# Sliding-window attention with a gated MLP on one core: q and k of batches 2 to 7 in runs of eight rows, sorted by VectorE, turned by one DMA transpose each

## The chip, the cores and the metric

The kernel runs on one core of a Trainium2 chip. The time is the device time of one execution in microseconds. A core has five engines that each run their own program in order: TensorE (in the profile PE, its weight loads PEld), VectorE (DVE), ScalarE (ACT), GpSimd (POOL) and SyncE (SP). They wait for each other through semaphores. DMA transfers are issued from SP, ACT or GpSimd and run on 16 DMA engines that all queues share.

## What is computed

q, k and v are 8 x 8 x 576 x 64 (batches, heads, rows, head size). Attention looks back over a window of 64 rows; its output, as 4608 rows of 512, goes through a two-layer MLP whose hidden values h become h * cos(h).

```
scores = scale * np.matmul(q, k.transpose(0, 1, 3, 2))
rel = pos[:, None] - pos[None, :]
mask = (rel >= 0) & (rel < window)
scores = np.where(mask, scores, -1000000000.0)
...
attn = np.exp(scores)
attn = attn / (np.sum(attn, axis=-1, keepdims=True) + 1e-09)
return np.matmul(attn, v).astype(np.float32)
...
h = x @ w_in
g = h * np.cos(h)
return (g @ w_out).astype(np.float32)
```

w_in is 512 x 2048, w_out 2048 x 512.

## The kernel before

**Tiles.** The MLP runs in nine macro tiles (mt 0 to 8) of 512 rows. Each has an h phase, in which PE makes 16 blocks of 128 hidden features (h_ps, four matmuls each, L458), ACT takes the sine (L597) and DVE multiplies h by it into gT (L600), and an out phase of 64 matmuls (out_ps, L611) whose results are copied and stored. The h blocks go round five PSUM banks, so a block's bank is taken again five blocks later. Attention works on batches of 576 rows; a batch has nine blocks j of 64 queries, each against 128 keys (block j - 1 and block j), and four pairs of heads. In tile mt the scores of batch mt + 1 are made, so that their results are there when the next tile takes its attention output (o_ps, values) as xT, the MLP's input.

**A batch's way.** For batches 2 to 7, `load_chunk` (L162) loads q and k on GpSimd's queue in six chunks of 96 rows for all heads, casting to bf16. `turn_k` (L238) turns each k chunk with a DMA transpose on SP's queue into kT, which holds head dimension on partitions and rows in order along the free axis. q is turned by PE: `transposed` (L193, L203) writes tq_ps in PSUM, one transpose of 96 columns per chunk and pair, and `put_q` (L213) has DVE copy it into qT. For batches 4 to 6 two of the six q chunks, and for batch 7 all six, go by DMA instead (`turn_q`, L226, `TURNED`, L40). `burst_scores` (L275) then issues the scores of several groups at once: 72 matmuls a batch (L289) in two bursts, of 32 and 40. The rhs is k as `keys` (L270) cuts it out; for even j the two chunks of 64 keys are read in reverse order. After that a group of four units goes through DVE (add of the mask with a minimum, L326), ACT (exp, L338), DVE (reciprocal, L348), GpSimd (the product w, L355) and a DMA transpose of w on SP's queue (L374; a few groups are transposed by PE, L371).

**Batches 0 and 1** are loaded by `load_heads` in runs of nine rows and turned by PE; their reordering is done when PSUM is copied. They and tile 0 are written out by hand in a list of steps (`FIRST`, L44 to L63), which also sets the first loads of batch 2 (Lq2, Lk2).

**The order of the rest** is a plan: `at(time, function, ...)` (L482) enters a step, and `pump(time)` (L485) emits all steps that are due. Time counts in units: tile mt begins at T * mt with T = 32, the h phase has units 0 to 15 (one per block), the out phase 16 to 31 (four matmuls each). The bursts are due at units 14.6 and 20.2 (the very first at 15.5), the work on a score group follows its place in the burst, the xT copies (`put_x`) come from 31.2 on. Lines 510 to 531 enter the loads, turns and spreads of each batch. The engines execute what is emitted for them in this order, and a step that must wait holds up what stands behind it on its engine.

**The start.** `make_identity` (L546; GpSimd, masks.py) comes first, then the list: `io` (iota on GpSimd, L127), the loads of the first pair of heads over SP, the masks made by DVE (`mk`) and cast by ACT (`mc`), the casts of the first rows, and then GpSimd's loads of the other pairs (L149).

## Time and profile before

| | us |
|---|---|
| median of 3 runs | 305.95 |
| lowest and highest | 305.73, 306.08 |
| span of the profiled execution | 304.8 |

| DMA queue | packets | MB | share of 16 engines |
|---|---|---|---|
| q0, issued from GpSimd | 100192 | 18.06 | 80.8% |
| q1, issued from SP | 57808 | 22.66 | 40.7% |

The span runs from the first to the last instruction of one execution, and the time of a run is a little longer than it. An engine's busy time is the time in which it executes something; a row of the stage view gives a stretch, its length and the busy time of each engine with the count of its instructions. The chain of waits follows the end of the program back to its start: each piece has its start, its length and the work that the rest waited for. A row of the group view has line, engine, operation, output and inputs with shapes, a count, then busy time in us and mean ns of one, then idle time of the engine just before and what ended it.

### The profile page before, as it was taken

How to read it: one execution, taken by the hardware profiler on the slowest of the kernel's cores; microseconds unless marked ns; L12 is line 12 of the kernel's file. 1: busy time of each engine (PE TensorE's matmuls, PEld its weight loads, DVE VectorE, ACT ScalarE, POOL GpSimd, SP SyncE). 2: the span in 40 equal slices, each digit the busy share in tenths (PEclk: the TensorE clock that was granted, in tenths of full speed). 3: DMA queues.
4: the chain of work that ended last, by engine and by line, in shares of the span. 5: the costliest groups of instructions: out<-in, count | busy, mean ns of one | idle time of the engine just before them, and what ended most of it. 6: DMA issues, size and time to landing. Idle time of an engine off the chain costs nothing.

```text
span 304.8 us, 8261 instructions
## 1 busy us (share of the span) xinstructions
PE 293.2 (96%) x2840; PEld 154.4 (51%) x2840; DVE 217.4 (71%) x868; ACT 233.7 (77%) x783; POOL 195.8 (64%) x226
## 2 busy tenths in 40 slices
PE   3789999999999999999999999999999999999995
PEld 3667854644455445444544444444544454454443
DVE  3797888898888877787678867886778677236701
ACT  5998699878986799779976998699869986116500
POOL 8899568986999579985998599769804930000000
PEclk9999999999999999999999999999999999999999
DMA  7999999999979995999999999999996852011011
GB/s 144 175 203 184 196 189 142 103 132 169 232 115 115 228 147 80 106 153 233 133 116 150 223 138 109 128 235 148 107 123 147 139 120 98 0 71 69 3 69 69
DMA packets 158186, 41.44 MB, mean 136 GB/s; under 512 B 146944, under 2 KB 153408, under 8 KB 158144
## 3 DMA queue, kind: packets, MB, share of 16 engines
q0 software_dynamic: 100192, 18.06, 80.8%
q1 hardware_dynamic: 57808, 22.66, 40.7%
q8 instruction: 22, 0.36, 0.5%
q14 instruction: 20, 0.16, 0.2%
q10 hardware_dynamic: 144, 0.20, 0.2%
HBM read 36.70 MB, written 9.44 MB: 151 GB/s over the span
## 4 chain that ended last, share of the span: by engine, by line
PE 90%; DVE 3%; DMA 2%; POOL 2%; ACT 1%; issue 1%; POOLq 0%
PE h_ps L458 37%; PE out_ps L611 36%; PE out_ps L441 5%; PE h_ps L422 4%; PE s_ps L289 3%; PE o_ps L390 3%; DMA k<-in_k_dram 2%; PE tq_ps L203 1%; PE out_ps L470 1%; DVE negm L321 1%; POOL q L149 1%; PE s_ps L311 1%; POOL k L149 1%; ACT e L338 0%; DVE wT L121 0%
## 5 line engine op out<-in xcount | busy, mean ns | idle before, releaser
L458 PE MATMUL h_ps<-xT,w_in 128*128 128x512 bf16 x512 | 115.1, 379 | 0.2
L611 PE MATMUL out_ps<-w_out,gT 128*128 128x512 bf16 x496 | 110.0, 379 | 0.0
L600 DVE TENSOR_TENSOR gT<-h_ps,sin 128x512 bf16<-128x512 f32 x128 | 85.1, 688 | 29.3 <-ACT sin L597 28.7
L338 ACT ACTIVATE e<-s,negm 128x128 f32<-128x128 f32 (+1 forms) x256 | 97.2, 382 | 1.7 <-POOL v L121 1.0
L597 ACT ACTIVATE sin<-h_ps 128x512 f32<-128x512 f32 x128 | 73.8, 598 | 31.4 <-PE h_ps L458 30.8
L355 POOL TENSOR_TENSOR w<-e,rden 128x512 bf16<-128x512 f32 (+1 forms) x68 | 69.3, 1033 | 30.8 <-DVE rden L348 25.0
L458 PEld LDWEIGHTS <-w_in 128*128 128x128 bf16 x512 | 48.9, 98 | 54.7
L611 PEld LDWEIGHTS <-gT 128*128 128x128 bf16 x496 | 47.4, 98 | 56.1
L326 DVE CUSTOM_DVE_ANT_0 s<-s_ps,mask 128x128 f32<-128x128 f32 (+1 forms) x256 | 56.1, 277 | 1.7 <-PE s_ps L311 1.4
L338 ACT ACTIVATION_READ_ACCUMULATOR e<-s,negm 128x1 f32 x256 | 48.3, 189 | 0.0
L172 POOL DMA_DIRECT2D v<-in_v_dram x40 | 34.1, 870 | 1.0 <-DMA q<-in_q_dram 1.0
L166 POOL DMA_DIRECT2D q<-in_q_dram x36 | 28.7, 797 | 7.6 <-DMA v<-in_v_dram 2.5
L166 POOL DMA_DIRECT2D k<-in_k_dram x36 | 28.5, 792 | 6.4 <-DMA k<-in_k_dram 4.5
L121 ACT COPY out_sb<-out_ps 128x512 f32<-128x512 f32 (+1 forms) x16 | 9.0, 563 | 23.9 <-PE out_ps L611 18.4
L348 DVE RECIPROCAL rden<-den 128x4 f32<-128x4 f32 (+1 forms) x73 | 12.2, 167 | 19.4 <-ACT e L338 19.0
L121 POOL COPY v<-v 64x1536 bf16<-64x1536 bf16 (+3 forms) x16 | 22.9, 1433 | 0.4
L121 DVE COPY out_sb<-out_ps 128x512 f32<-128x512 f32 x20 | 13.7, 687 | 12.1 <-PE out_ps L611 12.0
L121 DVE CAST xT<-o_ps 128x512 bf16<-128x512 f32 x24 | 15.6, 679 | 8.6 <-PE o_ps L390 8.4
L326 DVE DVE_READ_ACCUMULATOR2_ANT negm<- 128x1 f32 x256 | 21.3, 83 | 0.1
L441 PE MATMUL out_ps<-w_out,gT 128*128 128x512 bf16 x64 | 14.8, 380 | 0.0
L422 PE MATMUL h_ps<-xT,w_in 128*128 128x256 bf16 x128 | 14.6, 273 | 0.0
L422 PEld LDWEIGHTS <-w_in 128*128 128x128 bf16 x128 | 12.3, 98 | 1.4
(67 smaller groups left out, 230.9 us busy)
## 6 DMA issues: line engine op xcount, KB each, us to landing
out_dram<-out_sb SPq DMA_DIRECT2D x16, 512.0 KB, 7.3
v<-in_v_dram POOLq DMA_DIRECT2D x32, 128.0 KB, 6.0
q<-in_q_dram POOLq DMA_DIRECT2D x36, 96.0 KB, 8.7
k<-in_k_dram POOLq DMA_DIRECT2D x36, 96.0 KB, 8.6
w_in<-in_moe_w_in_dram POOLq DMA_DIRECT2D x4, 512.0 KB, 9.2
w_out<-in_moe_w_out_dram POOLq DMA_DIRECT2D x4, 512.0 KB, 11.0
q<-in_q_dram POOLq DMA_DIRECT2D x7, 144.0 KB, 6.5
k<-in_k_dram POOLq DMA_DIRECT2D x7, 144.0 KB, 6.7
```

What stands on the lines that cost most here:

```text
L121: {"a": nc.scalar.copy, "p": nc.gpsimd.tensor_copy}.get(engine, nc.vector.tensor_copy)(out, in_)
L166: nc.gpsimd.dma_start(out=st[name, b][:, c].rearrange("p (h d) -> p h d", h=H), in_=src.rearrange("h p d -> p h d"))
L172: nc.gpsimd.dma_start(out=vt.rearrange("p (h d) -> p h d", h=H), in_=v[b, :, c * 128:c * 128 + n, :].rearrange("h p d -> p h d"))
L326: nc.vector.tensor_tensor_reduce(out=s[:, u, c], in0=s_ps[:, u, c], in1=mask[:, 2 - j % 2 if j else 0, c], scale=-scale if b else -1.0, sc ...
L338: nc.scalar.activation(e[:, u, c], s[:, u, c], AF.Exp, bias=negm[:, u:u + 1], scale=1.0 if n < n_first else -1.0, accum_out=den[:, u:u + 1])
L355: (nc.gpsimd if engine == "p" else nc.vector).tensor_tensor(out=w[:, 0:u], in0=e[:, 0:u], op=ALU.mult, in1=rden[:, 0:u].unsqueeze(2).to_br ...
L422: nc.tensor.matmul(out=h_ps[:, half * e:half * e + half], lhsT=w_in_sb[:, ks, ff * 128:ff * 128 + 128], rhs=st["xT", 0][:, ks, half * g:ha ...
L441: nc.tensor.matmul(out=st["out", m], lhsT=st["g", ff // 2][:, ff % 2, m * 128:m * 128 + 128], rhs=w_out_sb[:, ff], start=ff == 0, stop=ff ...
L458: nc.tensor.matmul(out=st["h", ff], lhsT=w_in_sb[:, ks, ff * 128:ff * 128 + 128], rhs=st["xT", mt][:, ks], start=start, stop=stop)
L597: nc.scalar.activation(sin, h_ps, AF.Sin, bias=math.pi / 2.0)
L600: nc.vector.tensor_tensor(out=gt[:, e], in0=h_ps, in1=sin, op=ALU.mult)
L611: nc.tensor.matmul(out=o_ps[e], lhsT=gT[ff // 2][:, ff % 2, ms * 128:ms * 128 + 128], rhs=w_out_sb[:, ff], start=ff == 0, stop=ff == n_ff - 1)
```

## The change

- `load_chunk` gives way to `load_runs`: q or k of a batch is loaded in two parts of four heads, each partition taking eight successive rows of a head (72 partitions, 2 KB of the source in one piece).
- `sort_runs` (new, DVE): each part is copied into sorted_rows, 80 partitions by 8 by 512, so that the free axis goes first over the row's place in its run, then over heads and head dimension. Partitions 64 to 79 are zeroed once, on GpSimd.
- `turn` (new, SP): one DMA transpose turns all of sorted_rows (80 x 4096). k's result is kT itself, now [128, 8, 4, 80]: place in the run, pair, run. q's result is q_turned, a new tile with one buffer.
- `put_runs` (new, GpSimd): four copies a batch put q in row order into qT.
- `keys` and the burst's matmul: k is read in the order place in the run, then run (eight neighbouring elements, then a step of 320), and the output is written with a step of eight elements to put the columns in order.
- The PE transposes and copies of q for batches 2 to 7, `turn_q`, `turn_k` and `TURNED` are gone. Loads, sorts, turns, put_runs and the loads of v have new places in the plan; batches 2 and 3 have places of their own.

```diff
-NC, NP = 6, 96
+RUN, NP = 8, 80
+RUNS = (0.8, 0.6), (22, 9), (23.3, 10.3)
+RUNS3 = (1, 7), (28.4, 22), (29.5, 23.3)
-TURNED = {4: 2, 5: 2, 6: 2, 7: 6}
...
-    "Lq2.0 Ge.11 Gi.10 Gm.14 g.1.7 Lq2.1 Lq2.2 o.0.1.2 ...
+    "Lq2.0 Ge.11 Gi.10 Gm.14 g.1.7 Lq2.1 o.0.1.2 ...
...
-    "X.3.d Gm.18 o.3.3 oc.3.d Ge.18 Gn.17.d Lk2.4 Gi.18 Gn.18.d Lk2.5 Lv1.4 "
+    "X.3.d sq.0 sq.1 uq Gm.18 o.3.3 oc.3.d Ge.18 Gn.17.d Gi.18 Gn.18.d Lv1.4 "
...
+    sorted_rows = const.tile([NP, RUN, d_model], BF16, name="sorted_rows")
...
-    def load_chunk(name, b, c):
-        if (name, b) not in st:
-            st[name, b] = rows_tile(name)[0:NP].rearrange("p (c x) -> p c x", c=NC)
-        src = {"q": q, "k": k}[name][b, :, c * NP:c * NP + NP]
-        nc.gpsimd.dma_start(out=st[name, b][:, c].rearrange("p (h d) -> p h d", h=H),
-                            in_=src.rearrange("h p d -> p h d"))
+    def load_runs(name, b, part):
+        n = H // 2
+        st[name, b, part] = rows = rows_tile(name)[0:S // RUN, 0:n * RUN * D].rearrange("p (h x) -> p h x", h=n)
+        src = {"q": q, "k": k}[name][b, n * part:n * part + n]
+        nc.gpsimd.dma_start(out=rows, in_=src.rearrange("h (p r) d -> p h (r d)", r=RUN))
+
+    def sort_runs(name, b, part):
+        n = H // 2
+        to = sorted_rows[0:S // RUN, :, n * D * part:n * D * part + n * D]
+        nc.vector.tensor_copy(to.rearrange("p r (h d) -> p r h d", h=n),
+                              st.pop((name, b, part)).rearrange("p h (r d) -> p r h d", r=RUN))
...
-        else:
-            for c in range(TURNED.get(b, 0) if name == "q" else 0, NC):
-                nc.tensor.transpose(t_ps[:, NP * c:NP * c + NP], of[:, c, 128 * p:128 * p + 128], ident[:NP, :NP])
...
-    def turn_q(b, c):
-        nc.sync.dma_start(out=qsets[b % 2][:, :, c * NP:c * NP + NP], in_=st["q", b][:, c], transpose=True)
+    def turn(name, b):
+        if name == "k":
+            to = k_tile(b)
+        else:
+            st["q", b] = to = att.tile([128, RUN, PAIRS, NP], BF16, tag="q_turned", name="q_turned", bufs=1)
+        nc.sync.dma_start(out=to.rearrange("d r a x -> d (r a) x"), in_=sorted_rows.rearrange("p r x -> p (r x)"), transpose=True)
+
+    def put_runs(b, p):
+        of = st["q", b][:, :, p, 0:S // RUN]
+        nc.gpsimd.tensor_copy(qsets[b % 2][:, p].rearrange("d (x r) -> d x r", r=RUN), of.rearrange("d r x -> d x r"))
...
-            st["kA", b] = ka = att.tile([128, PAIRS, S], BF16, tag="kT", name="kT", bufs=2)
+            st["kA", b] = ka = att.tile([128, RUN, PAIRS, NP], BF16, tag="kT", name="kT", bufs=2)
...
-    def turn_k(b, c):
-        nc.sync.dma_start(out=k_tile(b)[:, :, c * NP:c * NP + NP], in_=st["k", b][:, c], transpose=True)
...
+        if b > 1:
+            rhs = st["kT", b, p][:, :, lo // RUN:lo // RUN + 64 // RUN * chunks]
+            rhs = rhs.rearrange("d r (a t) -> d a r t", a=chunks)
+            return rhs[:, ::-1] if j and j % 2 == 0 else rhs, chunks
...
-                        nc.tensor.matmul(out=to.rearrange("p (a t) -> p a t", a=chunks),
+                        nc.tensor.matmul(out=to.rearrange("p (a t r) -> p a r t", a=chunks, r=RUN),
...
-        for c in range(TURNED.get(b, 0)):
-            at(t0 - T + (24.3 if b == 4 else 23.4 if c < 2 else 26.4) + 0.01 * c, turn_q, b, c)
-        for p in range(PAIRS if TURNED.get(b) != NC else 0):
-            t_q = t0 + (2 if b == 2 else 1) + (3.3 if b == 2 else 3.5) * p
-            at(t_q, tr_q, b, p)
-            at(t_q + 0.02, put_q, b, p)
         if b > 2:
-            for c in range(NC):
-                for i, name in enumerate(("q", "k")):
-                    at(t0 - T + (17.9 + 2.8 * i if b == 3 and c == NC - 1 else 5.6 + 1.6 * c + 0.8 * i), load_chunk, name, b, c)
-        for c in range(NC):
-            at(t0 + 0.1 * c - (2 if b == 2 else 6), turn_k, b, c)
+            loads, sorts, turns = (RUNS3 if b == 3 else RUNS)
+            for i, name in enumerate("qk"):
+                for part in range(2):
+                    at(t0 - T + loads[i] + 0.1 * part, load_runs, name, b, part)
+                    at(t0 - T + sorts[i] + part, sort_runs, name, b, part)
+                at(t0 - T + turns[i], turn, name, b)
+        for p in range(PAIRS):
+            at(t0 + (7 if b == 2 else 5 if b == 3 else 3.3) + p, put_runs, b, p)
         for c in range(5):
-            at(t0 + (8 if TURNED.get(b) == NC else 0.5) + c, load_v, b, c)
+            at(t0 + 7.6 + c, load_v, b, c)
...
+    for part in range(2):
+        at(T + 5.4 + part, sort_runs, "k", 2, part)
+    at(T + 6.5, turn, "k", 2)
...
     make_identity(nc, ident)
     nc.vector.memset(small, 0.0)
+    nc.gpsimd.memset(sorted_rows[64:NP], 0.0)
     exp_table()
```

In this notation t0 = T * (b - 1) is the tile in which batch b's scores are made, and t0 - T the one before it.

More of the change, by code (lines that the diff above doesn't have):

```diff
@@ L195, in transposed, with in_order @@
         of = st[name, b]
-        if b < 2:
-            for c in range(RC):
-                for h in range(2):
-                    d = slice(64 * h, 64 * h + 64)
-                    nc.tensor.transpose(t_ps[d, 64 * c:64 * c + 64], of[d, p, 64 * c:64 * c + 64], ident[d, d])
-        else:
-            for c in range(TURNED.get(b, 0) if name == "q" else 0, NC):
-                nc.tensor.transpose(t_ps[:, NP * c:NP * c + NP], of[:, c, 128 * p:128 * p + 128], ident[:NP, :NP])
-        return t_ps
-    def in_order(t_ps, to, b):
-        return (t_ps.rearrange("d (c p) -> d p c", c=RC), to.rearrange("d (p c) -> d p c", c=RC)) if b < 2 else (t_ps, to)
+        for c in range(RC):
+            for h in range(2):
+                d = slice(64 * h, 64 * h + 64)
+                nc.tensor.transpose(t_ps[d, 64 * c:64 * c + 64], of[d, p, 64 * c:64 * c + 64], ident[d, d])
+        return t_ps
+    def in_order(t_ps, to):
+        return t_ps.rearrange("d (c p) -> d p c", c=RC), to.rearrange("d (p c) -> d p c", c=RC)
     def tr_q(b, p):
@@ L213, in put_q @@
     def put_q(b, p, engine=None):
-        if b > 1:
-            lo = TURNED.get(b, 0) * NP
-            copy(engine, qsets[b % 2][:, p, lo:], st.pop(("tq", b, p))[:, lo:])
-            return
-        of, to = in_order(st.pop(("tq", b, p)), qsets[b][:, p], b)
+        of, to = in_order(st.pop(("tq", b, p)), qsets[b][:, p])
         if b:
@@ L570 @@
              "c": lambda p, g, engine: g_put(2 * p + g, engine), "v": values_half, "x": put_x_half,
-             "tb": sine_table, "tb2": exp_table, "h": first_half, "S": sine_half, "g": gate_half,
+             "sq": lambda part: sort_runs("q", 2, part), "uq": lambda: turn("q", 2), "tb": sine_table, "tb2": exp_table, "h": first_half, "S": sine_half, "g": gate_half,
              "Gs": g_scores, "Gm": g_max, "Ge": g_exp, "Gi": g_inv, "Gn": g_norm, "Gw": g_trans, "Gc": g_trans,
```

15 lines of the change are left out of this document (8 added, 7 removed), and 6 rows, old and new, of the table FIRST.

## The prediction

> **What bounds the kernel now.** I read the page's engine shares first, then the busy time by stage, then the chain of waits, then the instruction groups with their shapes kept apart. A stage here is one macro tile: from its first h_ps matmul to the next tile's.
>
> ```profile
> span 304.8 us, 8261 instructions
> PE 293.2 (96%) x2840; PEld 154.4 (51%) x2840; DVE 217.4 (71%) x868; ACT 233.7 (77%) x783; POOL 195.8 (64%) x226
> ```
>
> ```profile
> core 0: us, PE busy (x) PEld busy (x) DVE busy (x) ACT busy (x) POOL busy (x), PEclk, DMA share, GB/s
> 57.50:89.30 31.80, 31.80 (x297) 15.89 (x295) 27.35 (x120) 27.12 (x100) 27.31 (x32) 1.00 1.99 163
> 89.30:120.80 31.50, 31.48 (x288) 15.59 (x289) 23.97 (x111) 27.28 (x95) 25.39 (x29) 1.00 1.41 140
> ...
> 152.00:183.20 31.20, 31.15 (x280) 15.27 (x281) 23.66 (x111) 27.10 (x95) 25.92 (x29) 1.00 1.58 155
> ...
> 214.40:244.90 30.50, 30.44 (x265) 14.57 (x265) 22.87 (x107) 27.09 (x95) 16.78 (x17) 1.00 0.92 127
> ```
>
> PE fills each tile and its clock is full, so a microsecond taken from PE in a tile is a microsecond gained, and any other engine matters only once it makes PE wait. The last row is tile 7, whose batch already has no q transpose on PE: 30.50 us, where tile 5 (with 16 of them) takes 31.20. That is the change's own experiment, made within the kernel before. The chain of waits says the same, and shows a second thing, the start:
>
> ```profile
> 0.78 0.18 POOL ident masks.py:197
> 0.96 0.07 issue
> 1.02 0.29 POOL ident masks.py:199
> 1.31 0.20 POOL mask L127
> ...
> 1.80 0.70 POOL q L149
> ...
> 5.87 6.71 DMA k<-in_k_dram
> ...
> 27.64 10.59 PE h_ps L422 x96
> ...
> 60.12 0.26 PE tq_ps L203 x6
> ...
> 85.13 0.22 PE tw_ps L371 x4
> ...
> 154.75 0.17 PE tq_ps L203 x4
> ...
> 166.68 0.52 PE s_ps L289 x32
> ...
> 172.48 0.80 PE s_ps L289 x40
> 173.28 8.74 PE out_ps L611 x40
> ```
>
> Until 5.87 us the chain is GpSimd alone, in its program's order: identity, iota, loads. From 26 us on it is almost only PE. So a delay at the head of GpSimd's program is carried to the end, because nothing behind it has slack. The last row also gives the planner's unit (four out_ps matmuls): 8.74 / 10 = 0.87 us.
>
> **The change part by part.** The rows that carry prices:
>
> ```profile
> L203 PE MATMUL tq_ps<-ident,q 96*128 96x96 bf16 x96 | 7.4, 205 | 0.0
> L121 DVE COPY qT<-tq_ps 128x576 bf16<-128x576 bf16 x12 | 6.4, 544 | 0.0
> L121 DVE COPY qT<-tq_ps 128x384 bf16<-128x384 bf16 x12 | 4.2, 347 | 0.0
> L121 DVE COPY v<-v 64x2048 bf16<-64x2048 bf16 x1 | 1.1, 1124 | 0.0
> L121 POOL COPY v<-v 64x512 bf16<-64x512 bf16 x2 | 2.0, 1012 | 0.1
> L166 POOL DMA_DIRECT2D q<-in_q_dram x36 | 28.7, 797 | 7.6 <-DMA v<-in_v_dram 2.5 <-PE tk_ps L200 1.6 <-DMA q<-in_q_dram 1.4
> L149 POOL DMA_DIRECT2D q<-in_q_dram x7 | 4.0, 578 | 0.5 <-DMA q<-in_q_dram 0.5
> masks.py:197 POOL MEMSET ident<- 128x128 bf16 x1 | 0.2, 205 | 0.3 <-POOLq L635 0.3
> L635 POOL MEMSET const-bfloat16-1.0<- 128x1 bf16 x1 | 0.1, 102 | 0.0
> L600 DVE TENSOR_TENSOR gT<-h_ps,sin 128x512 bf16<-128x512 f32 x128 | 85.1, 688 | 29.3 <-ACT sin L597 28.7
> L597 ACT ACTIVATE sin<-h_ps 128x512 f32<-128x512 f32 x128 | 73.8, 598 | 31.4 <-PE h_ps L458 30.8
> ```
>
> *Transposes removed from PE.* All 96 of L203 go. On the chain six take 0.26 us and four 0.17, so 0.043 us each: 96 x 0.0433 = **-4.16 us**. The stage rows agree: 31.20 - 30.50 = 0.70 for 16.
>
> *A memset added at the head of GpSimd's program.* The 16 spare partitions of sorted_rows, 4096 bf16 each, are zeroed right behind the identity, ahead of iota and every load. The two memset rows give (205 - 102) / 127 = 0.81 ns per element of a partition, so 0.10 + 4096 x 0.81 ns = 3.4 us. Lower end 0.1 us (the one-element row, if length cost nothing), upper end 6.6 (205 / 128 ns for each element). I take 3.4, since the 128-element row is this very operation, with this type, on this engine. DVE's masks wait for the iota, q's and k's first casts are queued behind them, and PE for both; every load shifts too. Nothing covers it: **+3.4 us**.
>
> *Loads.* Twelve chunk loads per batch at 0.797 become four; with 0.58 (the L149 row, long runs as well) GpSimd saves 9.6 - 2.3 = 7.3 us per batch. GpSimd's queue is not on the path after the start, so this earns nothing.
>
> *put_runs.* Four copies of 128x576 per batch on GpSimd. No row has its stepped read; the nearest copy takes 1.01 us at 512 elements, so some 1.1, and 2.2 at twice that. 4 x 1.1 = 4.4 us, less than the loads give back. It runs at units 3.3 to 6.3 and the scores come at 14.6, so 8 units (7 us) cover it; at 2.2 each it ends some 9 us after its start at unit 3.3, still before 14.6. Without that cover a score burst would wait. Nothing in the sum, 0 to +1 in the range.
>
> *Sorts on DVE.* Four copies of 72x2048 per batch replace four copies of qT. The nearest row is v's 64x2048: 1.12 us. DVE gains 4.5 and loses 1.4 (4 x 0.347) per tile, 23.7 + 3.1 = 26.8 of 30.5. In the h phase DVE gates each h_ps block.
>
> ```profile
> 160.09 0.69 DVE L600 TENSOR_TENSOR gT<-h_ps,sin 128x512 bf16<-128x512 f32 x1 [0.17 <-ACT sin L597]
> ```
>
> The block's bank (one of five) is needed again 4 x 0.87 = 3.5 us after PE leaves it; sin takes 0.60, the gate 0.69, with some 0.2 between, so slack is about 2.0 us. A k pair at units 9 and 10 delays by 2 x 1.12 less the 0.26 per block by which DVE is faster (0.60 apart against 0.87): 1.7. It fits, barely, so nothing in tiles 2 to 6.
>
> The Trainium skill, "VectorE: DVE Perf Modes", the tier table, gives a bf16 copy within SBUF four elements per cycle, 693 ns for 2048 elements. By that the pair would be far inside the slack; this trace's 2048 row took 1124 ns and does not show the faster rate.
>
> *Turns.* SP gets two large transposes for the six of k and the q chunks.
>
> ```profile
> kT<-k SPq DMA_TRANSPOSE x36, 5.0
> ```
>
> ```profile
> L239 SPq DMA_TRANSPOSE kT<-k x36: 1182/1216/2490, 59.3 to 228.2; - x36
> ```
>
> ```profile
> q1 hardware_dynamic: 57808, 22.66, 40.7%
> ```
>
> One turn moves 80 x 4096 x 2 = 655 KB. q1 moved 22.66 MB in 40.7% of 16 engines' 304.8 us, 183 KB per us with all of them, so 3.6 us of data. Issue on SP: at least 1.2 us, at most 9.7 if it goes by column blocks (32 against four). Landing after issue: 5.0 us (the chunk's median, which already holds queueing), 12 at worst. Queued behind the turn on SP are weight transposes and stores; the q turn of batch 4 stands ahead of the transpose of batch 3's block 4 (unit 24.2), due at 31, so there 0 taken, +4 in the range. In the steady tiles the sorted_rows buffer is reused 11.7 and 17.7 units (10 and 15 us) after a turn, so DVE does not wait. Two places are tight:
>
> ```profile
> 59.16 0.69 DVE L355 TENSOR_TENSOR w<-e,rden 128x512 bf16<-128x512 f32 x1
> 60.86 2.48 DVE L600 TENSOR_TENSOR gT<-h_ps,sin 128x512 bf16<-128x512 f32 x4 [1.00 <-ACT sin L597]
> ```
>
> Tile 1: batch 2's q sorts come right before it, 2.2 us on a DVE that has 1.0 us to spare; the first gate slips 1.2, of which some 0.6 is slack (PE asks for the first bank again around 62.1, the gate ends at 61.5). The k sorts at units 5.4 and 6.4 find DVE already late: 0.3 more. **+0.9 us** (0 to 3: batch 2's k turn at 6.5 is due at 15.5, 7.8 us). End of tile 1: batch 3's k turn goes out near unit 24.4 and lands 5.0 us, 5.8 units, later, at 30.2; the q sort placed at 28.4 needs the buffer and waits, then both sorts take 2.6 units, to 32.8. The xT copies behind them, due from 31.5, are 1.3 units late: **+1.1 us** (0 to 5).
>
> *Scores with strides.* 72 matmuls per batch read k in 16-byte runs and write every eighth PSUM column. They take 0.52 + 0.80 = 1.32 us per batch, 18 ns each since four run side by side. No row has a stepped access on PE. Lower end: nothing. Upper end: each alone, as the w transposes of the same 128 columns run (0.22 / 4 = 55 ns): 72 x 37 ns = 2.7 us per batch, 16 in all. I take nothing: the row nearest in kind is the same burst, where even blocks already read the two chunks in reverse with no price visible.
>
> The Trainium skill, "PSUM — Partial Sum Buffer", Specifications (TRN2), says the opposite: PSUM's lines are 8 bytes and any non-contiguous pattern slows matmuls significantly. No run here shows it yet; it gives no figure, and what it would do is the second rival.
>
> **Sum.** -4.16 + 3.4 + 0.9 + 1.1 = +1.2 us, on the span 304.8: 306.0. The runs' median lies 305.95 - 304.8 = 1.15 above the profiled span, so **307.2 us**, with 305.0 to 309.0 as this case's own range.
>
> **The rivals.**
>
> First, *the start absorbs the memset* (the other side). If the memset is far shorter than its length says, or the first loads catch up because fewer transfers stand beside them, the shift is near nothing: 307.2 - 3.4 = 303.8, and 302 where the tight places hold too. It decides once the shift is below 1.5 us. For it: the first two loads come over SP and do not shift. Against: the chain's first 5.9 us run through GpSimd without a gap.
>
> Second, *stepped scores stream at half rate.* The place is every burst, on PE. Doubled, they cost 1.32 x 6 = 7.9 more: 315.1; with only half of that 311. For it: nothing hides it, since PE is full. Against: only that no row shows a price. This is what the PSUM page's sentence would come to here.
>
> Third, *the sorts make PE wait in every tile.* If a sort also waits for its load or for the buffer, by 3 us where the slack left is 0.3 to 2, each of tiles 2 to 6 loses some 1.2: 313. For it: DVE is at 26.8 of 30.5 and the k pair almost uses up the slack. Against: 10 us between uses of the buffer.
>
> **How the numbers follow.** About 0.2% (0.6 us) is what this kernel's measurement can tell from no change. The forecast has 0.42 (0.03 faster, 0.12 within, 0.27 slower), the first rival 0.28 (0.26 faster, 0.02 within), the second 0.22 and the third 0.08 (all slower). That makes 0.29 faster, 0.14 the same, 0.57 slower. The range 302.6 to 312.5 leaves out a start that costs nothing beside tight places that hold, and the full doubling of the scores.
>
> **What would show it.** The first GpSimd load starts at 5.2 us and not 1.8 (memset right); PE's steady row after the start begins some 3 us later. Tiles 2 to 6 take 30.5 us each with no s_ps growth; 31.8 each would be the doubled score burst, visible as 1.0 and 1.6 us pieces on the chain. An idle DVE with a DMA as releaser at the end of tile 1, or an h_ps matmul waiting for DVE in tile 1, shows the two stalls. I am wrong if the memset is short, if strides cost PE, or if the sorts hold back gates in steady tiles.

## The result and the profile after

The changed kernel takes 348.36 us (median of 4 runs, 345.64 to 350.51), the kernel before 305.98 beside it: 1.137 times as long, with a 95% interval of 1.133 to 1.141. That is 42 us slower, where 1.2 were forecast and the range ended at 312.5. Executions of one version can lie some per cent apart at a lower granted clock, so where they lie more than 1.5% apart the faster ones are read: 347.72 us (and not 357.09) for e6, 327.82 (and not 334.46) for e11, 318.31 and 319.00 (and not 326.64 and 328.27) for e13.

First the page of the kernel after, its span and engine shares, and the shares of its chain of waits:

```profile
span 347.3 us, 7972 instructions
PE 303.7 (87%) x2744; PEld 157.4 (45%) x2744; DVE 226.7 (65%) x872; ACT 233.8 (67%) x783; POOL 191.7 (55%) x203
...
PE 37%; DMA 36%; POOL 11%; issue 5%; DVE 5%; ACT 4%; DVEq 0%; POOLq 0%
```

PE was 96% busy before and is 87% busy now; the program's end is set by transfers as much as by PE. PE also has 10.5 us more busy time for fewer instructions, to which the clock and the step in PSUM come back below. The view by stage, each row from a tile's first h_ps matmul to the next tile's (tiles mt 1, 2 and 6; the prediction called mt 4 "tile 5" and mt 6 "tile 7", and from here on the program's own numbers stand):

```profile
core 0: us, PE busy (x) PEld busy (x) DVE busy (x) ACT busy (x) POOL busy (x), PEclk, DMA share, GB/s
60.10:113.20 53.10, 36.05 (x273) 17.30 (x272) 30.80 (x128) 28.06 (x101) 23.57 (x24) 0.90 0.95 111
113.20:151.59 38.39, 31.99 (x264) 15.54 (x264) 26.45 (x111) 27.25 (x96) 24.81 (x25) 1.00 1.20 156
...
255.57:287.43 31.86, 31.62 (x265) 15.36 (x265) 22.95 (x107) 28.45 (x100) 24.18 (x23) 1.00 0.65 101
```

Subtracting the same stages of the kernel before gives where the 42.5 us between the two spans come from: the start +2.7, tile 1 +21.1, tile 2 +6.9, tiles 3 to 6 +3.6, +2.9, +4.0 and +1.3, and nothing in tiles 7 and 8, which no longer make scores. Half of the loss is in one tile. The chain of waits of the kernel after shows what is in it (start, length, work):

```profile
1.37 3.50 POOL sorted_rows L558
5.44 0.69 POOL q L151
...
60.92 14.61 DMA q_turned<-sorted_rows
75.62 0.69 DVE sorted_rows L173
76.31 0.61 DVE gT L611
76.97 1.10 PE h_ps L467 x3
78.06 12.31 DMA kT<-sorted_rows
90.41 1.71 PE s_ps L298 x32
...
269.88 0.89 PE s_ps L298 x32
...
276.06 1.43 PE s_ps L298 x40
```

Read it from 60.92. Batch 2's q turn takes 14.61 us. VectorE's sort of k needs the same buffer and stands in DVE's program ahead of gates; it can start at 75.62. The gate behind it, and the h_ps matmuls that want its bank, wait with it. Then k's turn goes out at 78.06 and lands 12.31 us later, and only then can the scores begin. The view of waits of the kernel after (engine, line, what it waited for: us in total, times, longest) shows that these waits are everywhere that a turn's end is needed:

```profile
POOL qT L234 <- DMA q_turned<-sorted_rows: 18.2, 2, 13.6
DVE sorted_rows L173 <- DMA kT<-sorted_rows: 16.6, 5, 4.6
...
PE h_ps L467 <- DVE gT L611: 10.1, 4, 5.2
...
PE s_ps L298 <- DMA kT<-sorted_rows: 8.2, 1, 8.2
...
DVE sorted_rows L173 <- DMA q_turned<-sorted_rows: 6.6, 1, 6.6
```

GpSimd's wait of 13.6 us stands in tile 1 too: `put_runs` waits for the q turn, and batch 3's k loads and batch 2's v loads are queued behind it. They go out from 77.3 us on, so they run beside the k turn of 78.06: one late turn makes the next one late. The turns themselves, by the transfer rows of the kernel after (median us from issue to landing) and by the view of their line (ns to issue one on SP: least, median, most):

```profile
q_turned<-sorted_rows SPq DMA_TRANSPOSE x6, 5.9
kT<-sorted_rows SPq DMA_TRANSPOSE x6, 13.8
```

```profile
L230 SPq DMA_TRANSPOSE q_turned<-sorted_rows x6: 3203/3426/6222, 60.9 to 251.1; - x6
L230 SPq DMA_TRANSPOSE kT<-sorted_rows x6: 3404/6416/8818, 78.1 to 235.2; - x6
...
DMA to landing us min/median/max: 5.6/10.7/15.6
```

The twelve turns, set beside the times at which GpSimd's loads are issued and land, fall into groups. Five have none of these loads beside them, or only the end of one, and land in 5.6 to 5.9 us. Six have four to seven of them beside them and land in 12.3 to 15.6. One (113.3 us), whose four loads start 1.6 us after it, takes 9.1. It isn't a matter of q or k: batch 3's k turn (103.85, no load beside it) takes 5.8, batch 2's q turn 14.6.

### The profile page after: what moved, and what is told of

The parts are those of the page before. It is cut to its first block, busy times and chain, and to the rows that moved or that the text cites. A ratio compares the mean times of both kernels' runs of the same rounds, so it can differ in the third digit from the quotient of the medians.

```text
span 347.3 us, 7972 instructions
## 1 busy us (share of the span) xinstructions
PE 303.7 (87%) x2744; PEld 157.4 (45%) x2744; DVE 226.7 (65%) x872; ACT 233.8 (67%) x783; POOL 191.7 (55%) x203
## 4 chain that ended last, share of the span: by engine, by line
PE 37%; DMA 36%; POOL 11%; issue 5%; DVE 5%; ACT 4%; DVEq 0%; POOLq 0%
PE h_ps L467 16%; PE out_ps L622 14%; DMA kT<-sorted_rows 13%; DMA k<-in_k_dram 7%; DMA w_out<-in_moe_w_out_dram 6%; DMA v<-in_v_dram 5%; DMA q_turned<-sorted_rows 4%; ACT e L347 4%; POOL w L364 4%; PE out_ps L450 3%; POOL v L123 2%; DVE sorted_rows L173 2%; PE s_ps L298 2%; PE out_ps L479 1%; POOL sorted_rows L558 1%
## 5 line engine op out<-in xcount | busy, mean ns | idle before, releaser
L467 PE MATMUL h_ps<-xT,w_in 128*128 128x512 bf16 x512 | 117.7, 391 | 12.3 <-DVE gT L611 10.1
L622 PE MATMUL out_ps<-w_out,gT 128*128 128x512 bf16 x496 | 110.9, 382 | 0.0
L611 DVE TENSOR_TENSOR gT<-h_ps,sin 128x512 bf16<-128x512 f32 x128 | 83.3, 686 | 29.7 <-ACT sin L608 29.6
L608 ACT ACTIVATE sin<-h_ps 128x512 f32<-128x512 f32 x128 | 73.4, 599 | 41.4 <-PE h_ps L467 34.9
L467 PEld LDWEIGHTS <-w_in 128*128 128x128 bf16 x512 | 51.3, 100 | 76.2 <-issue 20.4
L234 POOL COPY qT<-q_turned 128x576 bf16<-128x576 bf16 x24 | 28.8, 1247 | 18.2 <-DMA q_turned<-sorted_rows 18.2
L179 POOL DMA_DIRECT2D v<-in_v_dram x40 | 35.6, 901 | 1.0 <-DMA k<-in_k_dram 0.5
L123 DVE COPY out_sb<-out_ps 128x512 f32<-128x512 f32 x20 | 13.7, 686 | 15.1 <-PE out_ps L622 14.5
L298 PE MATMUL s_ps<-kT,qT 64*64 64x128 bf16 (+1 forms) x432 | 15.5, 312 | 8.2 <-DMA kT<-sorted_rows 8.2
L173 DVE COPY sorted_rows<-q 72x2048 bf16<-72x2048 bf16 x12 | 9.4, 819 | 16.6 <-DMA kT<-sorted_rows 16.6
L357 DVE RECIPROCAL rden<-den 128x4 f32<-128x4 f32 (+1 forms) x73 | 12.0, 165 | 11.4 <-ACT e L347 11.0
L399 PE MATMUL o_ps<-wT,v 128*64 128x64 bf16 x512 | 11.0, 197 | 8.6 <-POOL v L123 3.6
L298 PEld LDWEIGHTS <-qT 64*64 64x64 bf16 x432 | 12.2, 141 | 13.2 <-issue 13.2
## 6 DMA issues: line engine op xcount, KB each, us to landing
q<-in_q_dram POOLq DMA_DIRECT2D x12, 288.0 KB, 11.4
```

The source lines that it names most:

```text
L123: {"a": nc.scalar.copy, "p": nc.gpsimd.tensor_copy}.get(engine, nc.vector.tensor_copy)(out, in_)
L173: nc.vector.tensor_copy(to.rearrange("p r (h d) -> p r h d", h=n), st.pop((name, b, part)).rearrange("p h (r d) -> p r h d", r=RUN))
L179: nc.gpsimd.dma_start(out=vt.rearrange("p (h d) -> p h d", h=H), in_=v[b, :, c * 128:c * 128 + n, :].rearrange("h p d -> p h d"))
L234: nc.gpsimd.tensor_copy(qsets[b % 2][:, p].rearrange("d (x r) -> d x r", r=RUN), of.rearrange("d r x -> d x r"))
L298: nc.tensor.matmul(out=to.rearrange("p (a t r) -> p a r t", a=chunks, r=RUN), lhsT=qsets[b % 2][d, pe, 64 * j:64 * j + 64], rhs=rhs[d], st ...
L467: nc.tensor.matmul(out=st["h", ff], lhsT=w_in_sb[:, ks, ff * 128:ff * 128 + 128], rhs=st["xT", mt][:, ks], start=start, stop=stop)
```

## The experiments

A theory stood at the start: a turn lands in 12 to 15 us beside GpSimd's loads, and load, sort, turn and put form one chain through one buffer, which has no lead. The rivals were the memset, the stride on PE, and sorts that are simply too long. Each ratio is to the kernel before measured beside that run (306.85 to 307.37 us). The table has the length of each tile in us, worked out from the starts of the tiles' first h_ps matmuls in the traces.

| kernel | median us | tile 1 starts | 1 | 2 | 3 | 4 | 5 | 6 |
|---|---|---|---|---|---|---|---|---|
| before | 305.98 | 57.4 | 32.0 | 31.5 | 31.2 | 31.2 | 31.2 | 30.5 |
| after | 348.36 | 60.1 | 53.1 | 38.4 | 34.7 | 34.1 | 35.2 | 31.9 |
| e1_memset_late | 342.44 | 56.3 | 55.5 | 36.4 | 32.5 | 34.9 | 33.7 | 31.9 |
| e2_two_buffers | 336.20 | 59.8 | 45.3 | 37.9 | 31.5 | 31.5 | 37.8 | 31.5 |
| e3_no_v | 336.57 | 60.9 | 52.1 | 34.2 | 31.5 | 31.5 | 33.0 | 31.5 |
| e4_out_plain | 346.45 | 60.4 | 54.8 | 37.1 | 33.8 | 33.8 | 33.8 | 30.8 |
| e5_loads3_late | 332.76 | 60.1 | 43.0 | 36.2 | 32.9 | 31.5 | 34.2 | 31.9 |
| e6_read_steps | 347.72 | 60.2 | 54.6 | 35.9 | 33.8 | 33.9 | 33.9 | 33.6 |
| e7_v_first | 346.36 | 60.6 | 54.2 | 34.3 | 33.3 | 34.7 | 34.9 | 31.6 |
| e9_dve_order | 347.83 | 61.2 | 54.4 | 36.4 | 31.8 | 32.8 | 38.3 | 31.6 |
| e10_quiet_tile1 | 341.60 | 63.9 | 44.1 | 37.0 | 32.6 | 33.7 | 34.8 | 31.9 |
| e12_all | 326.19 | 58.5 | 41.0 | 38.2 | 30.5 | 33.2 | 33.0 | 30.5 |
| e13_lead | 318.31 and 319.00 | 59.1 | 35.1 | 36.5 | 31.1 | 32.7 | 31.6 | 30.5 |

**The memset later.** It moves from the head of GpSimd's program to behind the last load of w_out.

```diff
-    nc.gpsimd.memset(sorted_rows[64:NP], 0.0)
-    ... S.1.5 Lwo.3 h.1.7.4 ...
+    ... S.1.5 Lwo.3 z0 h.1.7.4 ...
+             "z0": lambda: nc.gpsimd.memset(sorted_rows[64:NP], 0.0),
```

> The memset of the spare partitions stands behind GpSimd's last w_out load, in a stretch where GpSimd was idle, and no longer ahead of iota. Theory (the start carries the memset through): the first GpSimd load starts at 1.8 us again instead of 5.4, tile 1 begins at 57.4 instead of 60.1, and the whole run gets 2.5 to 3.5 us shorter. Rival (the stalls of tile 1 come from transfers and swallow the shift): tile 1 begins earlier but ends as late as before, and the run changes by less than 1 us.

342.44 us, 1.116 times before (1.110 to 1.122). GpSimd's first load is back at 1.8 us, and tile 1 starts 3.8 us earlier, at 56.3, even ahead of the kernel before, so the memset's 3.5 us at the head were carried through the start in full. Tile 1 itself is longer by 2.4 (its q turn takes 17.27 us on the chain of this kernel), so at its end only 1.4 us of the gain are left: there the rival was nearly right. The whole run is 5.9 us shorter, more than the 2.5 to 3.5 expected; the rest comes from tiles 2 to 5, and why is open. The memset is a small part of the loss.

**Two buffers.** q and k each get a sorted buffer of their own; to make room s has five buffers and not six, wT 19 and not 20.

```diff
-    sorted_rows = const.tile([NP, RUN, d_model], BF16, name="sorted_rows")
+    sorted_of = {n: const.tile([NP, RUN, d_model], BF16, name=f"sorted_{n}") for n in "qk"}
...
```

> q and k are sorted into buffers of their own (s gets 5 buffers and wT 19 to make room; the second buffer is zeroed late on GpSimd). Theory A (the sort on VectorE waits until the other tensor's turn has left the one buffer, and TensorE waits for VectorE): the 16.6 and 6.6 us that the sorts wait for turns vanish, tiles 3 to 6 fall from 34.1 to 35.2 us to about 31.5 (30.5 plus the dearer score bursts), the run gets 14 to 20 us shorter. Rival B (the late transfer itself holds things up, by weight transposes behind it on SP and by k needed for the scores): the waits of the sorts vanish, but tiles 3 to 6 stay above 33 and the run gains under 8 us.

336.20 us, 1.096 times before (1.086 to 1.105), 12.2 less than the kernel after where 14 to 20 were expected. No sort waits for a turn any more, tile 1 loses 7.8 us of its excess, and tiles 3 and 4 run without a stall. What is left in tile 1 and in tile 5 is still the chain behind a load. The view of waits and, in tile 5, the chain of this kernel:

```profile
POOL qT L234 <- DMA q_turned<-sorted_q: 21.7, 2, 14.6
...
DVE sorted_k L173 <- DMA k<-in_k_dram: 6.9, 2, 3.6
...
PE s_ps L298 <- DMA kT<-sorted_k: 4.3, 1, 4.3
```

```profile
210.60 10.28 DMA k<-in_k_dram
```

With the buffer out of the way, the sort of k in tile 5 waits for its load, which takes 10.28 us, and PE waits for VectorE. So the shared buffer explains a part, and lateness passes on to the next member of the chain. Its two clean tiles, 31.5 us each, give the cost of the change without any stall: 0.3 us more than before's 31.2.

**Without v's loads.** The loads of v for batches 3 to 7 are left out; the attention of these batches uses older rows of v.

```diff
-        for c in range(5):
+        for c in range(5 if b == 2 else 0):
             at(t0 + 7.6 + c, load_v, b, c)
```

> The loads of v for batches 3 to 7 are left out (their output uses older rows of v); batch 2's stay. Theory B (the k turn lands late because v's loads of many short packets run beside it): kT's landing in tiles 2 to 6 falls from 13.8 us to about 6, the q sort waits under 3 us in all in these tiles, tiles 3 to 6 take about 31.5, the run gets 12 to 16 us shorter; tile 1 stays at 50 or more. Rival (the turn of k is slow by itself, by its size or by the weight transposes behind it): its landing stays over 10 us and the tiles at 34.

336.57 us, 1.097 times before (1.093 to 1.101), 11.8 less than the kernel after where 12 to 16 were expected. The transfer row of the k turn in this kernel:

```profile
kT<-sorted_rows SPq DMA_TRANSPOSE x6, 8.1
```

From 13.8 to 8.1 us by taking away loads that stood beside it: the length of a turn depends on what shares the DMA engines. It doesn't fall to the expected 6, since q's loads still stand beside k's turns. Tiles 3, 4 and 6 become clean; tile 1, where v2 and batch 3's loads remain, keeps 52.1, and its two turns still take 13.7 and 12.4.

**The step on the PSUM side.** The score matmuls write PSUM without a step, so the columns come out in another order than the mask's; k is still read in runs of eight.

```diff
-out=to.rearrange("p (a t r) -> p a r t", a=chunks, r=RUN),
+out=to.rearrange("p (a r t) -> p a r t", a=chunks, r=RUN),
```

> The score matmuls of batches 2 to 7 read k as in the changed kernel but write their columns one after the other, in another order (so the masked scores are of other keys; the work is the same). Theory C (the step on the PSUM side slows the matmuls): the clean bursts of tile 6 take 0.52 and 0.80 us again instead of 0.89 and 1.43, about 1.0 us per batch, so the run gets 3 to 6 us shorter. Rival (reading k in runs of 16 bytes slows them): the bursts stay at 0.89 and 1.43 and the run where it was.

**The step on the reading side.** The other way round: k element by element (a new 640-byte step for each), PSUM written without a step.

```diff
-            rhs = rhs.rearrange("d r (a t) -> d a r t", a=chunks)
+            rhs = rhs.rearrange("d r (a t) -> d a t r", a=chunks)
-out=to.rearrange("p (a t r) -> p a r t", a=chunks, r=RUN),
+out=to.rearrange("p (a t r) -> p a t r", a=chunks, r=RUN),
```

> The score matmuls of batches 2 to 7 write their columns one after the other and read k element by element with a step of 640 bytes (the columns come out in order). Theory C (only a step on the PSUM side costs): clean bursts take 0.52 and 0.80 us. Rival (a new 16-byte line for each element costs on the reading side): bursts of 0.9 and 1.4 us or more, up to three times the plain ones.

The two bursts of batch 7 (tile 6, where PE waits for no turn) on the chain, first without the PSUM step:

```profile
267.95 0.52 PE s_ps L298 x32
...
273.76 0.80 PE s_ps L298 x40
```

then with the element-wise read:

```profile
266.17 1.64 PE s_ps L298 x32
...
273.09 2.72 PE s_ps L298 x40
```

The kernel before took 0.52 and 0.80, the kernel after 0.89 and 1.43. So writing every eighth PSUM column costs 0.37 + 0.63 = 1.00 us a batch, 1.76 times the burst; reading k in 16-byte runs costs nothing; reading one element of each 16-byte run costs 4.36 - 1.32 = 3.0. The totals, 346.45 (1.129, 1.124 to 1.134) and 347.72, hardly show it: the first is 1.9 us below the kernel after, where 3 to 6 were expected and the bursts come to 6.0, and the second is no longer than the kernel after, though its bursts come to 12.2 us more. The stalls decide what reaches the end.

**Batch 3's loads later.** Only two times in the plan: batch 3's loads go from units 1 and 7 of tile 1 to 16 and 14, out of the way of batch 2's turns.

```diff
-RUNS3 = (1, 7), (28.4, 22), (29.5, 23.3)
+RUNS3 = (16, 14), (28.4, 22), (29.5, 23.3)
```

> Only the places of batch 3's loads change: q's from unit 1 to 16 and k's from 7 to 14 of tile 1, behind the two turns of batch 2. Theory B (a turn lands late because GpSimd's loads run beside it): batch 2's q turn lands in under 10 us instead of 14.6 and its k turn in under 9 instead of 12.3, and tile 1 takes 42 to 47 us instead of 53.1. Rival (these turns are slow because the start's other transfers, or their size, make them so): landings change by under 2 us and tile 1 stays above 50.

332.76 us, 1.085 times before (1.073 to 1.097), the largest gain of any single edit: 15.6 us after moving four transfers. Tile 1 falls from 53.1 to 43.0, within the 42 to 47 expected; the other 5.5 us are from tiles 2 to 5, whose plan is as before, and why is open. The chain of this kernel in tile 1:

```profile
72.77 7.80 DMA kT<-sorted_rows
```

k's turn in tile 1 took 12.31 us in the kernel after, and q's, 14.61 there, lands in 6.72. No work was removed, so the long landing comes from the loads beside the turn.

**v's loads first.** In batches 3 to 7, v goes ahead of k and q, whose sorts and turns come later too.

```diff
-RUNS = (0.8, 0.6), (22, 9), (23.3, 10.3)
+RUNS = (6.2, 5), (24, 14), (25.3, 15.3)
-            at(t0 + 7.6 + c, load_v, b, c)
+            at(t0 + (7.6 if b == 2 else 0.5) + c, load_v, b, c)
```

> From batch 3 on v is loaded first in its tile (unit 0.5 on), and for batches 4 to 7 k's loads follow at unit 5 and q's at 6.2, the k sort and turn at 14 to 15.3, the q sort and turn at 24 to 25.3. Theory B: with v's short packets gone before the k turn starts, kT lands in 6 to 9 us instead of 13.8 in tiles 2 to 5, the sorts wait under 3 us there in all, tiles 3 to 5 take 31.5 to 32.5 instead of 34.1 to 35.2. Rival (the long loads of q and k beside it do the same harm, or the sorts later in the tile hold VectorE at a worse place): landings above 10 and tiles above 33.5.

The transfer row and the waits of this kernel:

```profile
kT<-sorted_rows SPq DMA_TRANSPOSE x6, 6.2
```

```profile
POOL qT L234 <- DMA q_turned<-sorted_rows: 23.9, 5, 14.6
DVE sorted_rows L173 <- DMA k<-in_k_dram: 16.8, 8, 4.5
```

k's turns land in 6.2 us, as the theory has it, and the time is 346.36 (1.129, 1.118 to 1.141), as good as unchanged. DVE now waits 16.8 us for k's loads and GpSimd 23.9 for q's turns. In the kernel after DVE waited 2.2 us for k's loads and 16.6 for k's turns, which are 2.3 here. Tiles 3 to 5, expected at 31.5 to 32.5, take 33.3 to 34.9. A short landing earns nothing if the load ahead of it is as much later. What counts is the whole chain's lead.

**The order made by VectorE.** PSUM is written plain, in the order of the runs, and the masking operation (which reads PSUM anyway) reads with a step of 16 columns and writes in order.

```diff
-            rhs = rhs.rearrange("d r (a t) -> d a r t", a=chunks)
+            rhs = rhs.rearrange("d r (a t) -> d r a t", a=chunks)
...
-out=to.rearrange("p (a t r) -> p a r t", a=chunks, r=RUN),
+out=to.rearrange("p (r a t) -> p r a t", a=chunks, r=RUN),
...
+                if b > 1:
...
+                    of = of.rearrange("p (r x) -> p x r", r=RUN)
+                    to, m = (x.rearrange("p (x r) -> p x r", r=RUN) for x in (to, m))
...
```

> The score matmuls of batches 2 to 7 write PSUM without a step, columns ordered by place in the run and then run; VectorE's masking reads PSUM with a step instead and so puts them in order. Theory C: bursts of 0.52 and 0.80 us, tile 6 at 30.85 instead of 31.85. VectorE's mean for the masked step (274 ns) grows by 0 to 50 ns, which costs nothing on the path. Rival (VectorE's stepped reads become the limit of the burst's banks): bursts short, but tile 6 at 31.5 or more.

```profile
L339 DVE CUSTOM_DVE_ANT_0 s<-s_ps,mask 128x128 f32<-128x128 f32 x192 | 43.8, 280 | 1.6 <-PE s_ps L298 1.4
```

The group row of this kernel shows 280 ns for one; the kernel after has 281 for the unstepped form. So the order costs DVE nothing, with bursts of 0.52 and 0.79 us on PE. But tile 6 takes 31.6 us, which the rival gave as its sign (31.5 or more), and not 30.85. The stage view of this kernel has this tile:

```profile
254.88:286.46 31.58, 31.03 (x261) 14.83 (x265) 22.82 (x107) 27.97 (x99) 21.43 (x21) 0.97 0.66 97
```

PE waits under 1 us in it, and the granted clock is 0.97: it is 0.50 for the tile's first 2.2 us, behind waits of 0.8 and 1.1 us at the end of tile 5. So it isn't VectorE's stepped reads; the kernels of all parts below have the same reads and 30.5 in tile 6. The total, 347.83 (1.134, 1.123 to 1.145), again doesn't show the shorter bursts, because tiles 1, 2 and 5 wait for turns and loads.

**A quiet tile 1, by places alone.** Batch 2's k loads some 12 us earlier in the list, v2 at units 11 to 13, batch 3's loads at 16 and 14, its k sort and turn a unit later.

```diff
-RUNS3 = (1, 7), (28.4, 22), (29.5, 23.3)
+RUNS3 = (16, 14), (28.4, 23), (29.5, 24.3)
-            at(t0 + 7.6 + c, load_v, b, c)
+            at(t0 + (11 if b == 2 else 7.6) + (0.5 if b == 2 else 1) * c, load_v, b, c)
-    ... g.1.7 Lq2.1 o.0.1.2 ...
+    ... g.1.7 Lq2.1 Lk2.0 Lk2.1 o.0.1.2 ...
-    ... Gn.8.p Lk2.0 o.2.2 ... Gc.13 Lk2.1 Gp.8.d ...
+    ... Gn.8.p o.2.2 ... Gc.13 Gp.8.d ...
```

> Only places change: batch 2's k loads come right behind its q loads (some 12 us earlier), its v loads at unit 11 to 13 of tile 1 instead of 7.6 to 11.6, batch 3's q and k loads at 16 and 14, its k sort and turn one unit later. Theory B (tile 1's 21 us more are turns that land late beside GpSimd's loads, and what waits for them): q's turn of batch 2 lands in 6 to 8 us and k's too, tile 1 takes 33 to 37 us instead of 53.1 (43.4 with batch 3's loads late alone). Rival (the turns of the start are slow for another reason): tile 1 stays above 41.

341.60 us, 1.112 times before (1.099 to 1.126). A miss: tile 1 takes 44.1, about as with batch 3's loads alone (43.0), and the start is 3.8 us later: one of the moved k loads waits 2.9 us on GpSimd for PE's out_ps, with products queued behind it. Yet the turns land about as expected, q's in 6.7 us and k's in 8.3. The chain and the waits of this kernel have what is left:

```profile
76.18 8.26 DMA kT<-sorted_rows
```

```profile
PE s_ps L298 <- DMA kT<-sorted_rows: 5.0, 1, 5.0
```

k's turn goes out 12.2 us into the tile, and its 8.3 us don't fit before the scores. Loads out of the way are not enough.

**The parts together.** Two buffers, the memset late (on the same bytes seen as float32), the order on VectorE.

```diff
+             "z0": lambda: [nc.gpsimd.memset(sorted_of[n][64:NP].bitcast(F32), 0.0) for n in "qk"],
...
```

> Three parts together and no other place changed: two buffers for the sorted rows, their spare partitions zeroed late, PSUM written without a step and put in order by VectorE's masking. If the parts add up: start back at 57.4 or a little under, tile 1 at 43 to 46 (the late turns stay), tile 2 at 36 to 37, tiles 3 to 6 at 30.5 to 31, together 324 to 330 us. Rival (the parts share one wait, so that removing one uncovers another): above 333.

327.82 us in one execution, within the 324 to 330 expected if the parts add up. With the quiet tile 1 added, k's sort of the steady tiles at units 11 and 12 and its turn at 12.3:

```diff
-RUNS = (0.8, 0.6), (22, 9), (23.3, 10.3)
+RUNS = (0.8, 0.6), (22, 11), (23.3, 12.3)
```

> The three parts of the run before and the quiet tile 1, with the k sort of batches 4 to 7 at units 11 and 12 instead of 9 and 10. If all causes are found, every tile takes 30.5 to 31.5 us and the run 302 to 307 us. Rival (a cause is still missing, such as weight transposes behind the long turns on SP or loads that reach the sorts late): one or more tiles above 33, the run at 310 to 320.

326.19 us, 1.062 times before (1.055 to 1.069): above the 302 to 307 of the theory and also above the 310 to 320 of the rival. The rival is right that something was still missing: the chain of waits of this kernel names it.

```profile
70.69 8.57 DMA kT<-sorted_k
...
100.99 10.60 DMA q_turned<-sorted_q
```

Both turns are followed by the work that needs them (the view of waits has PE waiting 5.3 us for kT, and GpSimd 18.1 for q_turned in two places). They land sooner than the 12 to 15 us of the kernel after and are still late, so they go out too late.

**Lead.** The kernel of all parts, with batch 2's q sorted and turned before tile 1 begins, its k ahead of tile 1's first block, put_runs a unit later; batch 3's loads stand at units 10 and 11, its q is turned 6 units earlier and its k 2 units later.

```diff
-    ... Gn.16.d Gi.15 Gn.15.d ... Gw.15 Gp.15.d ... X.3.d sq.0 sq.1 uq Gm.18 ... Gn.18.d Lv1.4
+    ... Gn.16.d sq.0 sq.1 Gi.15 Gn.15.d ... Gw.15 uq Gp.15.d ... X.3.d Gm.18 ... Gn.18.d sk.0 sk.1 uk Lv1.4
-RUNS3 = (16, 14), (28.4, 23), (29.5, 24.3)
+RUNS3 = (10, 11), (22, 25), (23.3, 26.3)
...
```

> The kernel of two buffers, plain PSUM writes, late memset and quiet tile 1 (326.19 us), with nothing but lead added to the turns of batches 2 and 3: batch 2's q is sorted and turned before tile 1 begins, its k right behind the last product of the hand-written list (before the first block of tile 1, not at unit 6), its put_runs one unit later; batch 3's loads at units 10 and 11 of tile 1, q sorted at 22 and turned at 23.3, k sorted at 25 and turned at 26.3 (before: q's turn at 29.5). My theory (what is left in tiles 1 and 2 is landing time that had no lead): PE waits for kT under 1 us in tile 1 (5.3 before), tile 1 takes 33 to 36 us instead of 41.4, tile 2 33 to 35 instead of 38.6, 313 to 319 us in all. Rival (the order on DVE and ACT at the head of tile 1 and the weight transposes late on SP cost as much, wherever the turns stand): tile 1 stays at 39 or more, 323 or more.

318.31 and 319.00 us. Stages of tiles 1 and 2 of this kernel, and some of its waits:

```profile
59.12:94.23 35.11, 30.96 (x271) 15.08 (x273) 28.98 (x124) 27.81 (x101) 20.31 (x22) 1.00 1.29 147
94.23:130.74 36.51, 32.32 (x260) 15.51 (x263) 25.32 (x111) 27.12 (x94) 27.22 (x27) 0.92 1.26 164
```

```profile
POOL qT L234 <- DMA q_turned<-sorted_q: 6.6, 1, 6.6
...
PE o_ps L406 <- POOL v L123: 5.7, 2, 3.9
...
PE o_ps L406 <- DMA wT<-w: 4.4, 2, 3.7
```

PE no longer waits for kT at all; tile 1 takes 35.1 (expected 33 to 36), and the total is within the 313 to 319 expected. Tile 2 misses: 36.5 where 33 to 35 were expected. Its clock is 0.92, and the chain of this kernel enters it through a load of v:

```profile
71.90 18.92 DMA v<-in_v_dram
```

This is batch 2's v, issued behind put_runs and batch 3's k loads; its spread and the values come late. PE's waits of this kernel, put in order of time, say the same: 3.9 us for this spread at the end of tile 1, and half the clock for 3.4 us from the start of tile 2, behind it; then 3.7 at the end of tile 2 for a weight transpose, whose product stood on GpSimd behind the spread of batch 3's v; and 1.8 in tile 4 for a spread again. So most of what is left hangs on v, its loads and its spreads. Whether v is late because the turns were given the lead was not tried.

No version run here beats the kernel before. From the kernel after's span to this one 30.8 of 42.5 us are gone; of the 11.7 left, the start has 1.8, tile 1 3.1, tile 2 5.0, tile 4 1.5 and tile 5 0.4.

## Why the prediction was wrong

**The step that failed is the landing of a turn.** The prediction put it as "Landing after issue: 5.0 us (the chunk's median, which already holds queueing), 12 at worst", and took 5.0. That median is of a chunk of 98 KB; a turn moves 655 KB. It took 5.6 to 5.9 us without GpSimd's loads beside it, and 12.3 to 15.6 with them. The table of before held a warning: the packets of GpSimd's queue took 80.8% of the 16 engines' span and those of SP's 40.7%, more than the whole together, so the full rate behind the 3.6 us of data was not to be counted on. The worst case of 12 was written down, close to what came, and not carried through: a sort that needs the buffer 10 us after a turn was put at nothing, though 12 is more than 10.

**Two statements rested on that number and fell with it, and a third did not.**
- "In the steady tiles the sorted_rows buffer is reused 11.7 and 17.7 units (10 and 15 us) after a turn, so DVE does not wait": with k's turns landing in 13.7 to 15.6 us the q sort waits for them in each of tiles 2 to 5, 14.3 us in all. The two-buffer kernel takes exactly these waits away.
- Tile 1 at +0.9: it was +21.1. The forecast looked at DVE's 2.2 us of sorts; what decided was that q's turn, k's sort, k's turn and the scores follow one another through one buffer, 14.6 + 0.7 + 12.3 us and what lies between, in place of six chunks turned well ahead.
- "+1.1" at the end of tile 1 for batch 3's q sort came about as forecast: the turn it waits for landed in 5.8 us (5.0 taken), and DVE waits 2.3 us for it.

**The lead of the whole chain was not priced.** Only batch 2's k turn was set against its due time (7.8 us), with the landing of 5.0. Each tensor has to be loaded (7.0 us for k and 11.4 for q at the median), sorted, turned (5.6 to 15.6) and, for q, put, on three engines that execute in order. Before, an early chunk could be turned while the last was still loading. Moving v's loads shortened the turn and lengthened the wait for the load by as much; giving batches 2 and 3 more lead took 7 to 8 us more off a kernel that had every other part mended. That is shown; the rest of tiles 2 and 4 goes back to v by the trace, and that the turns' lead made v late is only argued.

**Strides on PE.** Taken at 0, with 2.7 us a batch as upper end. Measured 1.00 us a batch, 6.0 in all. The reason given for 0 (the reversed order of two chunks shows no price) says nothing of a step within a chunk. The step is on the write side alone; reading in 16-byte runs is free, as taken. This is three quarters of the second rival's doubling (1.00 of 1.32 us a batch). The Trainium skill, "PSUM — Partial Sum Buffer", Specifications (TRN2), which says that non-contiguous patterns slow matmuls, was right against the forecast; the price here is a factor of 1.76 for a step of 32 bytes.

**What was right.**
- The transposes: 0.70 us a tile less. The clean tiles of the two-buffer kernel, 31.5, are before's 31.2 less 0.70 plus the step's 1.00; with a plain PSUM write and two buffers tile 6 has 30.5, as it had before, when no q transposes were left in it.
- The memset, 3.4 us by the element rate, and that the start carries it:

```profile
L558 POOL MEMSET sorted_rows<- 16x4096 bf16 x1 | 3.5, 3504 | 0.1
...
L234 POOL COPY qT<-q_turned 128x576 bf16<-128x576 bf16 x24 | 28.8, 1247 | 18.2 <-DMA q_turned<-sorted_rows 18.2
```

These group rows of the kernel after also show put_runs at 1.25 us, forecast 1.1, and what put_runs costs beside its time: GpSimd's queue stands still behind it. The first load of GpSimd begins at 5.44 us, forecast 5.2. The first rival (the start absorbs it) is out.
- The sorts were priced too high, which hid nothing. The view of their line in the kernel after (ns for one: least, median, most):

```profile
L173 DVE COPY sorted_rows<-q x12: 673/686/2096, 59.6 to 250.4; 72x2048 bf16<-72x2048 bf16 x12
L173 DVE COPY sorted_rows<-k x12: 677/711/2486, 75.6 to 234.4; 72x2048 bf16<-72x2048 bf16 x12
```

0.69 and 0.71 us at the median, not 1.12, and near the 693 ns that the Trainium skill, "VectorE: DVE Perf Modes", the tier table, gives for 2048 elements. Seven of the 24 take 0.89 to 2.49 us; each of these runs beside work of GpSimd, as did the row of 1.12 us from the kernel before that the price was taken from. That GpSimd slows them is argued from this, not tried. So most of the sorts are not too long, as the third rival had it; but that rival's mechanism, a sort that "waits for its load or for the buffer", is the nearest to what happened. It was given 0.08, "against: 10 us between uses of the buffer", which is again the landing.

Without any stall the change would cost 6 x 1.00 - 4.16 + 2.7 at the start, some +4.5 us, about 310.5. That would have been within the range, though the sum had nothing for the step; the stalls are nine tenths of the result.

## What to carry to other kernels

When many small transfers become one, price the one beside everything that shares the DMA engines at that moment, and ask how early its input is whole: the latency of the chain load, rearrange, turn, use takes the place of the pieces' overlap. Put a wait of that length on each in-order engine that the chain crosses and look at what is queued behind it. If a number in the sum has a worst case that is twice its value, carry the worst case through every step that uses it.

## What the runs showed of the hardware

**A stall costs PE more than its length.** Windows of the kernel after, behind the longest wait in tile 1 and around a shorter one at the end of tile 4:

```profile
90.40:92.20 1.80, 1.79 (x33) 1.38 (x33) 0.91 (x11) 0.58 (x3) 0.00 (x0) 0.50 1.23 330
92.20:99.20 7.00, 7.00 (x32) 2.80 (x34) 3.53 (x32) 5.36 (x29) 2.55 (x3) 0.87 0.91 89
...
216.92:220.33 3.41, 1.35 (x65) 1.19 (x65) 2.88 (x19) 3.41 (x19) 3.27 (x3) 1.00 1.06 170
220.33:223.74 3.41, 3.36 (x11) 1.20 (x9) 1.29 (x4) 2.64 (x6) 3.41 (x5) 0.50 0.39 68
```

Behind the wait of 8.2 us (82.2 to 90.4) the granted clock is 0.50, until 94.0, and the first burst takes 1.71 us, where it takes 0.89 in tile 6. PE is busy for 36.1 us in this tile, before it was 31.9: some 4 us of the 21 are slow matmuls, not waiting (an estimate: the step adds 1.0 in this tile and the transposes that are gone take off about as much). The Trainium skill, "TensorE: Matmul & The Clock Gate", Part 1, has the clock at half after an idle window of about 3.4 us; the trace agrees in the half and in its lasting for microseconds. It differs in the wait: at 220.3 us the half clock follows a wait of 2.1 us, with PE busy for 1.35 of the 3.41 us before it, so here a shorter wait was enough.

**GpSimd's memset goes by elements, not bytes.** 16 x 4096 bf16 took 3.50 us; the same bytes as 16 x 2048 float32 took 1.80 in the kernels with all parts.

**Issuing a turn occupies SP for 3.2 us at least and up to 8.8** (the view of its line above), against 1.2 for a chunk of 96 rows at the median. The long ones are those beside loads: 3.2 to 3.5 us for the five turns that land in 5.6 to 5.9, 5.2 to 8.8 for the six that land in 12.3 to 15.6. Weight transposes and stores queue behind it on SP.

**Rearranging is free in some places.** VectorE's masking operation reads PSUM with a step of 16 columns in 280 ns as it does without in 281. PE reads 16-byte runs at full speed, but with one element per run its bursts take 3.3 times as long, and with a step of 32 bytes on the PSUM side 1.76 times.
